# Attention with a fused feed-forward and expert stage: joint transposed tile, paired selector sums, rope sums on another engine

## The chip, the cores and the metric

The kernel runs on one core of a Trainium2 chip. The metric is the device time of one execution in microseconds (us), lower is better. The engines are TensorE (PE in the rows, PEld its weight loads), VectorE (DVE), ScalarE (ACT), GpSimd (POOL) and SyncE (SP, which issues DMAs). Each has its own queue and works through it in order; semaphores hold an instruction until what it needs is there.

## The reference

Three stages follow one another. Only the first is touched; B=4, H=8, S=576, D=64 in fp32:

```
q_rot, k_rot = (rotate(q), rotate(k))           # x1*cos - x2*sin, x1*sin + x2*cos
scores = 1/sqrt(D) * matmul(q_rot, k_rot.T)
scores = scores - max(scores, axis=-1)
attn = exp(scores)
attn = attn / (sum(attn, axis=-1) + 1e-9)
x = matmul(attn, v)                             # 2304 tokens x 512 after the heads are joined
x = moe(x)                                      # RMS norm, silu(x w_gate) * (x w_val), w_out
out = moe2(x)                                   # one of 8 experts per token, relu, gate weight
```

## The kernel before

Attention works on 32 heads `i`, in 16 pairs `p`. A step `g` is one turn of a loop from -25 to 175; a head takes five steps, a pair ten. In each step the list `plan` (L52) is gone through in its order, and each entry (name, offset) calls its method for the head or pair whose time has come: offset -10 means ten steps before the head's first step. So the order of the list is the order of the instructions in every engine's queue within a step, and the offset says in which step. A head's 576 positions are handled as five blocks of rows `j` (four of 128, one of 64).

- `ropeA` multiplies q and k by cosine and sine on GpSimd; `ropeC` (L236) adds the two products, for q on GpSimd, for k on VectorE (`T["rc"]`); `ropeH` (ScalarE, L243) rounds the sum to fp32r, `ropeL` (VectorE, L248) takes the rest, so that both halves together are exact.
- `TQ` (L257) transposes q and k of one head on TensorE, ten transposes into the PSUM tiles `t1` (512 columns each of q and k) and `t2` (64 each). `TE` (L269) copies them to SBUF on ScalarE, k (512 and 64 columns, L274 and L275) and q in turn, and issues the DMAs that make kB and qB.
- `SM` (L286) is one block of scores, row maxima by a reduction on VectorE (L293). `QD` copies the upper half of q by DMA. `MT` (L299) transposes the maxima, ScalarE copies them to `mr`, and a DMA puts them as a row into qB.
- `ST` (L306) is one block of transposed scores, first kA with qA (L317), then kB with qB (L319), the row of maxima being part of qB; ScalarE's exponential (L320) writes it to `E`.
- `AV` (L325) multiplies E with v, `UE` copies the result out. `DN` (L344) sums E over its rows by products with selector matrices: one with `selh` and eight with `sel8`, each in four column tiles of 144 columns. `SQ` does the same for squares. `stat` adds the results, and now and then `wstep` emits small VectorE operations and GpSimd products (L486) that scale what a batch has finished (`ws1` says how many per step). `conv_part` splits weights of the next stage (`cp`).

The score tiles of SM and ST and the tile `t1` come from one PSUM pool, `psA`, with three buffers in rotation; `t2` and MT's tile come from `psC` with one. Before the change AV stands at offset 13 (fourth step of a head), DN at 18, TQ and the two TE in the step at offset -10, ahead of that step's ST.

Of the kernel before, what the change touches and what calls it, by code (L numbers as in the profile page):

```python
# [9 lines left out]
F32 = mybir.dt.float32  # L10
F32R = mybir.dt.float32r
# [6 lines left out]
ALU = mybir.AluOpType  # L18
# [3 lines left out]
B, H, S, D = 4, 8, 576, 64  # L22
NT, DM, DFF = 2304, 512, 1536
P = 128
NPAIR = B * H // 2
NHEAD = B * H
# [5 lines left out]
def fr(ap):  # L32
    return ap.bitcast(F32)
# [16 lines left out]

class Kernel:
    plan = (  # L52
        ("UE1", 20), ("UE0", 15), ("SM", -8), ("AV", 13), ("LV", 1), ("SQ", 23), ("ropeHq", -14), ("TQ", -10),
        ("ropeHk", -13), ("QD", -4), ("TEk", -10), ("ropeLq", -13), ("DN", 18), ("ropeAq", -22), ("ropeAk", -20),
        ("ropeLk", -13), ("LQ", -12), ("MT", -3), ("TEq", -10), ("ropeCk", -15), ("ropeCq", -17), ("ST", 0),
    )


# [207 lines left out]
                nc.tensor.transpose(o, src[:, h * 5 + j].rearrange("p e d -> p (e d)"), self.idr)  # L266
        self.st["t", i] = (t1, t2)

    def TE(self, i, nm):  # L269
        nc, st = self.nc, self.st  # L270
        t1, t2 = st["t", i]
        x = "qk".index(nm)
        dst = self.tp.tile([P, S], F32R, tag=nm + "T", name=nm + "T")
        nc.scalar.copy(dst[:, 0:512], fr(t1[:, x]))  # L274
        nc.scalar.copy(dst[:, 512:576], fr(t2[:, x * 128:x * 128 + 64]))  # L275
        st[nm + "A", i] = dst
        if nm == "q":
            qB = self.tp.tile([P, 640], F32R, tag="qB", name="qB")
            self.dm(qB[0:64, 0:576], dst[64:128])
            st["qB", i] = qB  # L280
        else:
            kB = self.kBt[i % 3]
            self.dm(kB[0:64], dst[0:64])
            st["kB", i] = kB

    def SM(self, i, j):  # L286
        nc = self.nc
# [46 lines left out]
    def UE(self, p, u):  # L334
# [6 lines left out]
            self.st["sq", p] = self.sm.tile([P, S], F32, tag="sq", name="sq")  # L341
        nc.scalar.activation(self.st["sq", p][:, 288 * u:288 * u + 288], av[:, :288], AF.Square)  # L342

    def DN(self, p):  # L344
        nc = self.nc
        b, hp = divmod(p, 4)
        E = self.st["E", p]
        d = self.side(p, 1)
        parts = [(self.selh[:, hp, :], E[:, 0, 4, :])]
        for h in range(2):  # L350
            parts += [(self.sel8[:, 2 * hp + h, :], E[:, h, j, :]) for j in range(4)]
        for x, (w, r) in enumerate(parts):
            for t in range(4):
                nc.tensor.matmul(d[32 * t:32 * t + 32, 0:144], w, r[:, 144 * t:144 * t + 144], start=(x == 0), stop=(x == 8), tile_position=(0, 32 * t))
        self.later.append((b, hp, 0, d))

    def SQ(self, p):
# [141 lines left out]
    def attention(self):  # L499
# [47 lines left out]
        def act(nm, off):  # L547
            if nm in ("UE0", "UE1"):
                ok(self.UE, at(g, off, 10), int(nm[2]))
            elif nm == "ST":  # L550
                ok(self.ST, *divmod(g - off, 5))
            elif nm in ("MT", "TQ", "QD"):
                ok(getattr(self, nm), lagged(nm, off, 5))
            elif nm[:2] == "TE":
                ok(self.TE, lagged("TE", off, 5), nm[2])
            elif nm == "DN":
                ok(self.DN, late(off, self.dnt))
                q = late(off + 1, self.dnt + 1)
                if q >= 0 and q % 4 == 3:
                    wq.append(self.W0(q // 4))  # L560
                if q == 14:
                    wq.append(self.Wa())
            elif nm == "SQ":
                q = late(off, self.sqt)
                ok(self.SQ, q)
                q = late(off + 1, self.sqt)
                if q >= 0 and q % 4 == 3:
                    wq.append(self.W(q // 4))
            elif nm == "SM":
                ok(self.SM, *divmod(g - off, 5))  # L570
            elif nm == "AV":
                if g >= 10 * NPAIR:
                    if g < 10 * NPAIR + 10:
                        self.AV(NPAIR - 1, *divmod(g - 10 * NPAIR, 5))
                elif (g - off) % 5 == 0:
                    p, y = divmod((g - off) // 5, 2)
                    for j in range(5):
                        ok(self.AV, p, y, j)
            elif nm == "LV":
                p = at(g, off, 10)  # L580
                if 0 < p < NPAIR:
                    self.loads(p, "v")
            elif nm == "LQ":
                p = at(g, off, 10)
                if 0 <= p < NPAIR - 2:
                    self.loads(p + 2, "qk")
            elif nm[:4] == "rope":
                ok(getattr(self, nm[:5]), roped(nm, off), nm[5])

# [288 lines left out]
SIZES = (128, 256, 288, 352, 384)  # L878


T = dict(wz=0, pi=8, ck="g", ck8="", c1=0, g0=70, cp=(0, 1, 1, 0, 1, 0, 1, 1, 0, 1), ws1=(0, 1, 2, 2, 1, 0, 1, 1, 2, 1), np=1, w4=3, p0=8, u0=-1, pp=[(1, 1), (1, 3), (2, 1), (2, 3), (3, 1), (3, 3)], w3=4, sqt=12, rc="q", dnt=7, ck2="g", ws=2, ws2=4, u2=1, c2=1, wy=0, yt={0: 1, 2: 1, 3: 2, 4: 1}, yr={0: 2, 2: 2, 3: 1, 4: 1}, bt={1: (0, 1), 2: (2, 2), 3: (3, 3), 5: (4, 5)}, yl={0: 1, 2: 1, 3: 1, 4: 2}, ba={0: (1, 2), 2: (1,), 3: (1,), 4: (1, 3, 5)})


class Ring:
# [752 lines left out]
```

## Time and profile before

| what | us |
|---|---|
| median of 3 runs (1128.01 to 1131.2) | 1130.47 |
| profiled execution | 1130.2 |
| its span, first to last instruction | 1128.4 |
| TensorE busy | 1048.8 (93%) |
| VectorE busy | 655.5 (58%) |
| ScalarE busy | 457.5 (41%) |
| GpSimd busy | 293.2 (26%) |

Attention fills the span from the start to about 350 us, and its last products lie between those of the next stage up to about 377 us. The views are: the page with the busy times; a table of busy time by stretch; the waits, who waited for whom; and the instructions of an engine in order of time. In the order of time a row is: start (us), duration (us), engine, line, operation, output<-input, partitions x elements, count, and in brackets idle time before it and what ended it. A duration runs into that of the next instruction where work is pipelined, so the distance between starts says what an instruction costs its queue.

### The profile page before, as it was taken

How to read it: one execution, taken by the hardware profiler on the slowest of the kernel's cores; microseconds unless marked ns; L12 is line 12 of the kernel's file. 1: busy time of each engine (PE TensorE's matmuls, PEld its weight loads, DVE VectorE, ACT ScalarE, POOL GpSimd, SP SyncE). 2: the span in 40 equal slices, each digit the busy share in tenths (PEclk: the TensorE clock that was granted, in tenths of full speed). 3: DMA queues.
4: the chain of work that ended last, by engine and by line, in shares of the span. 5: the costliest groups of instructions: out<-in, count | busy, mean ns of one | idle time of the engine just before them, and what ended most of it. 6: DMA issues, size and time to landing. Idle time of an engine off the chain costs nothing. (4 is left out here: it accounts for less than half of the span.)

```text
span 1128.4 us, 19271 instructions
## 1 busy us (share of the span) xinstructions
PE 1048.8 (93%) x7174; PEld 891.2 (79%) x7174; DVE 655.5 (58%) x1313; ACT 457.5 (41%) x1023; POOL 293.2 (26%) x357
## 2 busy tenths in 40 slices
PE   3999999999999899999999999999998998899895
PEld 3777777777676689899999999999886887798684
DVE  8554656675642866656565556563457855655653
ACT  2645655655555343322222222222234534434441
POOL 7553356266402401112011011110010132221211
PEclk9999999999998999999999999999999999999998
DMA  4433344335221201111113111100136655655553
GB/s 132 95 86 90 96 119 131 99 106 141 59 74 38 80 16 50 57 47 57 30 62 109 38 48 38 42 25 28 58 125 214 190 188 175 208 185 182 199 189 115
DMA packets 75713, 113.44 MB, mean 101 GB/s; under 512 B 18520, under 2 KB 43376, under 8 KB 75570
## 3 DMA queue, kind: packets, MB, share of 16 engines
q1 hardware_dynamic: 71890, 99.72, 30.1%
q0 software_dynamic: 3680, 11.91, 2.9%
q8 instruction: 78, 1.28, 0.5%
q14 instruction: 65, 0.53, 0.2%
HBM read 85.39 MB, written 12.17 MB: 86 GB/s over the span
## 5 line engine op out<-in xcount | busy, mean ns | idle before, releaser
L760 PE MATMUL gv<-xh,whi 128*128 128x384 f32 x576 | 198.4, 344 | 1.8 <-ACT xh L738 1.4
L760 PE MATMUL gv<-xl,whi 128*128 128x384 f32 x576 | 196.3, 341 | 3.3 <-POOL xl L742 3.1
L760 PE MATMUL gv<-xh,wlo 128*128 128x384 f32 x576 | 196.0, 340 | 0.4 <-POOL wlo L659 0.4
L293 DVE TENSOR_REDUCE m<-s 128x1 fp32r<-128x576 f32 (+1 forms) x160 | 119.9, 752 | 123.8 <-PE s L292 122.6
L320 ACT ACTIVATE E<-sT 128x576 f32<-128x576 f32 (+1 forms) x160 | 104.9, 659 | 137.5 <-PE sT L319 132.0
L659 POOL TENSOR_TENSOR wlo<-cvt,whi 128x256 fp32r<-128x256 f32 x66 | 50.6, 770 | 341.8 <-ACT whi L658 341.8
L770 DVE TENSOR_TENSOR s<-s,gv 128x384 f32<-128x384 f32 x72 | 39.8, 554 | 157.3 <-PE gv L760 150.0
L760 PEld LDWEIGHTS gv<-xh,whi 128*128 128x128 f32 x576 | 109.2, 190 | 8.1 <-issue 3.6
L760 PEld LDWEIGHTS gv<-xl,whi 128*128 128x128 f32 x576 | 109.4, 190 | 5.3 <-POOL xl L742 3.5
L769 ACT ACTIVATE s<-gv 128x384 f32<-128x384 f32 x72 | 34.9, 492 | 192.0 <-PE gv L760 191.9
L760 PEld LDWEIGHTS gv<-xh,wlo 128*128 128x128 f32 x576 | 109.3, 190 | 1.1 <-POOL wlo L659 1.0
L317 PE MATMUL sT<-qT,kT 128*128 128x288 f32 (+1 forms) x320 | 79.9, 332 | 13.0 <-ACT qT L274 13.0
L788 PE MATMUL yps<-whi,hh 128*128 128x512 f32 x216 | 87.3, 404 | 2.9 <-ACT yacc L793 1.4
L331 PE MATMUL av<-E,vraw 128*64 128x288 f32 x640 | 86.5, 414 | 0.8 <-ACT sq L342 0.8
L803 DVE TENSOR_TENSOR yacc<-yacc,yps 128x512 f32<-128x512 f32 x99 | 67.6, 686 | 31.8 <-PE yps L788 30.6
L788 PE MATMUL yps<-wlo,hh 128*128 128x512 f32 x216 | 85.3, 395 | 0.0
L788 PE MATMUL yps<-whi,hl 128*128 128x512 f32 x216 | 85.2, 394 | 0.0
L292 PE MATMUL s<-kT,qT 128*128 128x288 f32 (+1 forms) x320 | 78.2, 330 | 4.9 <-DVE m L293 2.7
L317 PEld LDWEIGHTS sT<-qT,kT 128*128 128x128 f32 (+1 forms) x320 | 47.8, 181 | 30.1 <-ACT qT L274 21.2
L1302 POOL DMA_INDIRECT x<-ysc,ix x27 | 33.0, 1221 | 144.8 <-DVE e L1128 76.7
L319 PE MATMUL sT<-qB,kB 65*128 65x288 f32 (+1 forms) x320 | 69.8, 300 | 0.0
L331 PEld LDWEIGHTS av<-E,vraw 128*64 128x64 f32 x640 | 42.7, 137 | 32.2 <-issue 6.5
(288 smaller groups left out, 1968.6 us busy)
## 6 DMA issues: line engine op xcount, KB each, us to landing
raw<-in_w SPq DMA_DIRECT2D x52, 512.0 KB
stt<-in_w SPq DMA_DIRECT2D x25, 512.0 KB
stt<-in_w_gate SPq DMA_DIRECT2D x24, 256.0 KB
stt<-in_w_val SPq DMA_DIRECT2D x24, 256.0 KB
stt<-in_w_out SPq DMA_DIRECT2D x24, 256.0 KB
kB<-kT SPq DMA_DIRECT2D x32, 144.0 KB
qB<-qT SPq DMA_DIRECT2D x32, 144.0 KB
qT<-qT SPq DMA_DIRECT2D x32, 144.0 KB
```

What stands on the lines that cost most here:

```text
L292: nc.tensor.matmul(s[:n, u, 0:288], qA[:, j * 128:j * 128 + n], kA[:, u * 288:u * 288 + 288], start=True, stop=True)
L293: nc.vector.tensor_reduce(m[:n, j:j + 1], s[:n, :, 0:288], axis=AX.XY, op=ALU.max)
L317: nc.tensor.matmul(s[:n, u, 0:288], kA[:, j * 128:j * 128 + n], qA[:, u * 288:u * 288 + 288], start=True, stop=False)
L319: nc.tensor.matmul(s[:n, u, 0:288], kB[0:65, j * 128:j * 128 + n], qB[0:65, u * 288:u * 288 + 288], start=False, stop=True)
L320: nc.scalar.activation(e.rearrange("p (u c) -> p u c", u=2), s[:n, :, 0:288], AF.Exp, scale=0.125)
L331: self.nc.tensor.matmul(av[64 * h:64 * h + 64, 0:288], V[:, h, j * 64:j * 64 + 64], E[:, h if j < 4 else 0, j, 288 * u:288 * u + 288], sta ...
L659: nc.gpsimd.tensor_tensor(lo, f, fr(hi), op=ALU.subtract)
L760: nc.tensor.matmul(t[:, :CH], w[:, k], r[:, k], start=(n == 0), stop=(n == 11))
L769: nc.scalar.activation(s, ps[0][:, :CH], AF.Silu)
L770: nc.vector.tensor_tensor(s, s, ps[1][:, :CH], op=ALU.mult)
L788: nc.tensor.matmul(ps, l, r[:, 2], start=(n == 0), stop=(n == tot - 1))
L803: nc.vector.tensor_tensor(old[:, t], old[:, t], ps, op=ALU.add)
```

## The change

q and k transposed of a head share one tile `qkT`, and TE makes two copies, of 2 x 512 and of 2 x 64 columns, instead of four. TQ and TE stand at the end of their step, behind ST. `EP` adds E blocks 0 and 1, and 2 and 3, of each head (`es=(0, 1)`; `eg=()` puts both on VectorE), and DN takes the two sums of a head instead of four blocks: five products instead of nine. AV moves from offset 13 to 12 and so ahead of MT and ST of the same step. The rope sum of k goes to GpSimd as that of q does (`rc="qk"`). Offsets and order of the other entries move by a step at most (ropeCk from -15 to -17), and `cp` and `ws1` are dealt out anew: `cp` sums to 6 as before, `ws1` to 13 instead of 11.

```diff
--- before.py
+++ after.py
@@ -50,9 +50,9 @@
 
 class Kernel:
     plan = (
-        ("UE1", 20), ("UE0", 15), ("SM", -8), ("AV", 13), ("LV", 1), ("SQ", 23), ("ropeHq", -14), ("TQ", -10),
-        ("ropeHk", -13), ("QD", -4), ("TEk", -10), ("ropeLq", -13), ("DN", 18), ("ropeAq", -22), ("ropeAk", -20),
-        ("ropeLk", -13), ("LQ", -12), ("MT", -3), ("TEq", -10), ("ropeCk", -15), ("ropeCq", -17), ("ST", 0),
+        ("UE1", 20), ("UE0", 15), ("SM", -8), ("AV", 12), ("SQ", 23), ("ropeCk", -17), ("ropeHk", -14), ("EP0", 10),
+        ("ropeCq", -18), ("QD", -4), ("ropeHq", -14), ("ropeAq", -22), ("EP1", 12), ("ropeLq", -13), ("DN", 18),
+        ("ropeAk", -21), ("ropeLk", -12), ("LQ", -11), ("LV", 1), ("MT", -3), ("ST", 0), ("TQ", -10), ("TE", -10),
     )
 
 
@@ -266,22 +266,17 @@
                 nc.tensor.transpose(o, src[:, h * 5 + j].rearrange("p e d -> p (e d)"), self.idr)
         self.st["t", i] = (t1, t2)
 
-    def TE(self, i, nm):
+    def TE(self, i):
         nc, st = self.nc, self.st
         t1, t2 = st["t", i]
-        x = "qk".index(nm)
-        dst = self.tp.tile([P, S], F32R, tag=nm + "T", name=nm + "T")
-        nc.scalar.copy(dst[:, 0:512], fr(t1[:, x]))
-        nc.scalar.copy(dst[:, 512:576], fr(t2[:, x * 128:x * 128 + 64]))
-        st[nm + "A", i] = dst
-        if nm == "q":
-            qB = self.tp.tile([P, 640], F32R, tag="qB", name="qB")
-            self.dm(qB[0:64, 0:576], dst[64:128])
-            st["qB", i] = qB
-        else:
-            kB = self.kBt[i % 3]
-            self.dm(kB[0:64], dst[0:64])
-            st["kB", i] = kB
+        dst = self.tp.tile([P, 2, S], F32R, tag="qkT", name="qkT")
+        nc.scalar.copy(dst[:, :, 0:512], fr(t1))
+        nc.scalar.copy(dst[:, :, 512:576], fr(t2[:, 0:256]).rearrange("p (x n) -> p x n", x=2)[:, :, 0:64])
+        st["qA", i], st["kA", i] = dst[:, 0], dst[:, 1]
+        kB = st["kB", i] = self.kBt[i % 3]
+        self.dm(kB[0:64], dst[0:64, 1])
+        qB = st["qB", i] = self.tp.tile([P, 640], F32R, tag="qB", name="qB")
+        self.dm(qB[0:64, 0:576], dst[64:128, 0])
 
     def SM(self, i, j):
         nc = self.nc
@@ -341,6 +336,14 @@
             self.st["sq", p] = self.sm.tile([P, S], F32, tag="sq", name="sq")
         nc.scalar.activation(self.st["sq", p][:, 288 * u:288 * u + 288], av[:, :288], AF.Square)
 
+    def EP(self, i, k):
+
+        if k not in T["es"]:
+            return
+        E = self.st["E", i // 2]
+        t = self.st["es", i, k] = self.sm.tile([P, S], F32, tag=f"es{k}", name=f"es{k}", bufs=2)
+        (self.nc.gpsimd if k in T["eg"] else self.nc.vector).tensor_tensor(t, E[:, i % 2, 2 * k, :], E[:, i % 2, 2 * k + 1, :], op=ALU.add)
+
     def DN(self, p):
         nc = self.nc
         b, hp = divmod(p, 4)
@@ -348,10 +351,12 @@
         d = self.side(p, 1)
         parts = [(self.selh[:, hp, :], E[:, 0, 4, :])]
         for h in range(2):
-            parts += [(self.sel8[:, 2 * hp + h, :], E[:, h, j, :]) for j in range(4)]
+            w = self.sel8[:, 2 * hp + h, :]
+            for k in range(2):
+                parts += [(w, self.st.pop(("es", 2 * p + h, k)))] if k in T["es"] else [(w, E[:, h, j, :]) for j in (2 * k, 2 * k + 1)]
         for x, (w, r) in enumerate(parts):
             for t in range(4):
-                nc.tensor.matmul(d[32 * t:32 * t + 32, 0:144], w, r[:, 144 * t:144 * t + 144], start=(x == 0), stop=(x == 8), tile_position=(0, 32 * t))
+                nc.tensor.matmul(d[32 * t:32 * t + 32, 0:144], w, r[:, 144 * t:144 * t + 144], start=(x == 0), stop=(x == len(parts) - 1), tile_position=(0, 32 * t))
         self.later.append((b, hp, 0, d))
 
     def SQ(self, p):
@@ -552,7 +557,7 @@
             elif nm in ("MT", "TQ", "QD"):
                 ok(getattr(self, nm), lagged(nm, off, 5))
             elif nm[:2] == "TE":
-                ok(self.TE, lagged("TE", off, 5), nm[2])
+                ok(self.TE, lagged("TE", off, 5))
             elif nm == "DN":
                 ok(self.DN, late(off, self.dnt))
                 q = late(off + 1, self.dnt + 1)
@@ -584,6 +589,12 @@
                 p = at(g, off, 10)
                 if 0 <= p < NPAIR - 2:
                     self.loads(p + 2, "qk")
+            elif nm[:2] == "EP":
+                q = at(g, off, 5)
+                if q >= NHEAD - 2 or q < 0:
+                    q = g - 10 * NPAIR - 1 + NHEAD - 2
+                    q = q if NHEAD - 2 <= q < NHEAD else -1
+                ok(self.EP, q, int(nm[2]))
             elif nm[:4] == "rope":
                 ok(getattr(self, nm[:5]), roped(nm, off), nm[5])
 
@@ -878,7 +889,7 @@
 SIZES = (128, 256, 288, 352, 384)
 
 
-T = dict(wz=0, pi=8, ck="g", ck8="", c1=0, g0=70, cp=(0, 1, 1, 0, 1, 0, 1, 1, 0, 1), ws1=(0, 1, 2, 2, 1, 0, 1, 1, 2, 1), np=1, w4=3, p0=8, u0=-1, pp=[(1, 1), (1, 3), (2, 1), (2, 3), (3, 1), (3, 3)], w3=4, sqt=12, rc="q", dnt=7, ck2="g", ws=2, ws2=4, u2=1, c2=1, wy=0, yt={0: 1, 2: 1, 3: 2, 4: 1}, yr={0: 2, 2: 2, 3: 1, 4: 1}, bt={1: (0, 1), 2: (2, 2), 3: (3, 3), 5: (4, 5)}, yl={0: 1, 2: 1, 3: 1, 4: 2}, ba={0: (1, 2), 2: (1,), 3: (1,), 4: (1, 3, 5)})
+T = dict(wz=0, pi=8, ck="g", ck8="", c1=0, g0=70, cp=(0, 2, 0, 0, 1, 0, 1, 1, 0, 1, ), ws1=(1, 1, 2, 3, 1, 0, 1, 1, 2, 1, ), np=1, w4=3, p0=8, u0=-1, pp=[(1, 1), (1, 3), (2, 1), (2, 3), (3, 1), (3, 3)], w3=4, sqt=12, rc="qk", es=(0, 1, ), eg=(), dnt=7, ck2="g", ws=2, ws2=4, u2=1, c2=1, wy=0, yt={0: 1, 2: 1, 3: 2, 4: 1}, yr={0: 2, 2: 2, 3: 1, 4: 1}, bt={1: (0, 1), 2: (2, 2), 3: (3, 3), 5: (4, 5)}, yl={0: 1, 2: 1, 3: 1, 4: 2}, ba={0: (1, 2), 2: (1,), 3: (1,), 4: (1, 3, 5)})
 
 
 class Ring:
```

## Rows read from the trace of the kernel before

**Rows 1.** The page: busy time of each engine, share, instructions.

```profile
PE 1048.8 (93%) x7174; PEld 891.2 (79%) x7174; DVE 655.5 (58%) x1313; ACT 457.5 (41%) x1023; POOL 293.2 (26%) x357
```

**Rows 2.** Stretches of one pair: length; PE, PEld, DVE, ACT, POOL; clock; DMA, GB/s.

```profile
83.80:104.60 20.80, 19.72 (x204) 14.90 (x202) 10.10 (x16) 11.64 (x28) 8.95 (x12) 1.00 0.36 87
...
230.20:251.20 21.00, 19.90 (x204) 14.87 (x202) 15.75 (x28) 12.17 (x30) 10.99 (x14) 1.00 0.41 106
...
272.10:293.10 21.00, 19.71 (x204) 14.86 (x202) 11.77 (x17) 12.16 (x30) 18.12 (x25) 1.00 0.28 70
```

**Rows 3.** Waits of TensorE from 62.7 to 314.3 us: total, times, longest.

```profile
PE sT L317 <- ACT qT L274: 11.1, 23, 0.9
PE s L292 <- DVE m L293: 1.8, 8, 0.4
```

**Rows 4.** TensorE in order of time, 200 to 224 us.

```profile
205.07 2.14 PE L354 MATMUL av<-E,sel 128*32 128x144 f32 x64
207.15 0.53 PE L317 MATMUL sT<-qT,kT 128*128 128x288 f32 x2
...
212.48 0.43 PE L292 MATMUL s<-kT,qT 128*128 128x288 f32 x2
212.74 0.22 PE L301 MATMUL t<-idr,m 128*8 128x128 f32 x1
...
213.83 2.65 PE L331 MATMUL av<-E,vraw 128*64 128x288 f32 x20
...
218.69 0.62 PE L266 MATMUL t<-idr,qhl 128*128 128x128 f32 x5
...
219.58 0.50 PE L317 MATMUL sT<-qT,kT 128*128 128x288 f32 x2
...
220.25 0.48 PE L292 MATMUL s<-kT,qT 128*64 128x288 f32 x2
220.94 0.53 PE L317 MATMUL sT<-qT,kT 128*128 128x288 f32 x2 [0.21 <-ACT qT L274]
```

**Rows 5.** VectorE's k sums (ns, min/median/max), the longest, and GpSimd beside it.

```profile
L236 DVE TENSOR_TENSOR A<-A,B x12: 811/815/1380, 73.4 to 303.8; 128x640 f32<-128x640 f32 x12
...
177.43 1.38 DVE L236 TENSOR_TENSOR A<-A,B 128x640 f32<-128x640 f32 x1
...
177.10 2.17 POOL L486 TENSOR_TENSOR x<-x,wb 128x384 f32<-128x384 f32 x2 [3.59 <-DMA wb<-wscr]
```

**Rows 6.** ScalarE in order of time, 200 to 224 us.

```profile
213.22 0.24 ACT L303 CAST mr<-t 8x128 fp32r<-8x128 f32 x1
...
219.70 0.58 ACT L274 CAST kT<-t 128x512 fp32r<-128x512 f32 x1
220.18 0.22 ACT L275 CAST kT<-t 128x64 fp32r<-128x64 f32 x1
...
220.86 0.70 ACT L320 ACTIVATE E<-sT 128x576 f32<-128x576 f32 x1
221.41 0.76 ACT L243 CAST qhl<-A 128x640 fp32r<-128x640 f32 x1
```

**Rows 7.** SP's queue and TensorE in order of time, up to 62 us.

```profile
40.21 0.73 SPq L197 DMA_DIRECT2D qB<-mr  x1
...
43.43 0.50 PE L317 MATMUL sT<-qT,kT 128*128 128x288 f32 x2
```

**Rows 8.** GpSimd's q sum and its reader on ScalarE, 260 to 310 us.

```profile
278.03 1.54 POOL L236 TENSOR_TENSOR A<-A,B 128x640 f32<-128x640 f32 x1
...
284.38 0.73 ACT L243 CAST qhl<-A 128x640 fp32r<-128x640 f32 x1
```

**Rows 9.** TensorE in order of time, up to 62 us.

```profile
26.16 0.85 PE L266 MATMUL t<-idr,qhl 128*128 128x128 f32 x5 [3.23 <-DVE qhl L248]
...
27.80 0.81 PE L317 MATMUL sT<-qT,kT 128*128 128x288 f32 x2
```

**Rows 10.** Busy time and granted clock in one stretch; columns as in rows 2.

```profile
355.00:360.00 5.00, 4.93 (x16) 3.90 (x16) 0.00 (x0) 3.26 (x7) 4.67 (x6) 0.53 0.00 0
```

## The prediction, made before the change was run

> **What bounds the kernel now.** I read the page's busy times first. TensorE is busy for 1048.8 us of 1128.4, 93%, and VectorE for 58% [rows 1]. That is a mean over stages, so the next view is the table by stretch, cut at the start of the transposes of every second head, so that one row is one pair of heads. A quiet pair (83.80 to 104.60) takes 20.80 us: TensorE 19.72, VectorE 10.10, ScalarE 11.64, GpSimd 8.95. The fullest pairs of the other engines are 230.20 to 251.20 (VectorE 15.75 of 21.0) and 272.10 to 293.10 (GpSimd 18.12 of 21.0) [rows 2]. All the change's edits lie in this stage, 16 pairs, and there TensorE is the bound; nobody else comes near except GpSimd in one stretch. The third view says what TensorE's remaining idle time is: in twelve pairs it waits 11.1 us, in 23 places, for the copies of q and k transposed (L274) and 1.8 us, in 8 places, for a maximum (L293) [rows 3]. The fourth, TensorE's order of time, gives prices as distances between starts, because durations overlap [rows 4]. After the attention stage the program is the same in both kernels, and TensorE sets it too; what the stage saves I carry to the end one for one.
>
> **The change part by part.** The sum is made against the profiled execution, 1130.2 us (1.8 over its span of 1128.4), which lies 0.3 under the median, 1130.47.
>
> *Selector products (DN).* Eight products with sel8, each of four tiles side by side, run from 205.07 to 207.15, 2.08 us [rows 4], so 0.26 each. Four of eight go: 1.04 us a pair, on TensorE's own queue with nothing to hide behind. 16 pairs: 16.6 us. In the last pair this lies between products of the next stage, and I count it as well.
>
> *The adds (EP).* 64 adds of 128x576 on VectorE. Not in the trace; the nearest row is the k sum, the same operation on 640 columns: 0.815 us at the median [rows 5], so by columns 0.73 (an estimate). Four a pair are 2.9 us, and the k sum that leaves makes it 2.1 net. 10.10 + 2.1 is 12.2 of about 19 us in a quiet pair, and 15.75 + 2.1 is 17.9 in the fullest [rows 2]. VectorE's queue is in order, so behind each add stands the maximum (L293) that frees a score buffer. The first add of a head stands in the step with the transposes, which give 0.89 us (218.69 to 219.58 [rows 4]) to cover 0.73; the second stands in the step of the AV products, 2.65 us (at 213.83 [rows 4]). DN itself waits for the add of the step before, with AV in between. So I price the adds at 0; without that cover they cost 64 x 0.73 = 47 us.
>
> *Transposes and copies at the end of the step.* Three score buffers rotate, and the transposes take one. Now the second score product behind them (ST of the next step) needs that buffer back; afterwards it is the third (SM of the step after that). In the row: ScalarE is free for the copies at 219.70, the four of them take until the exponential at 220.86, 1.16 us, and ST starts at 220.94, where TensorE was through with SM, which takes 0.26 (212.48 to 212.74), at 220.25 + 0.26 = 220.51 [rows 4, 6]. The stall is 0.43, of which the wait column shows 0.21: it hides about 0.2, so the 23 waits of 11.1 us [rows 3] are about 0.69 each. Afterwards the exponential goes first (0.55, 220.86 to 221.41 [rows 6]). Two copies of 1024 and 128 columns follow; with 0.58 for 512 columns and 0.22 for 64 [rows 6], 0.8 ns a column, the long one is an estimate of 1.0 us, and the buffer is free 0.55 + 1.0 + 0.05 = 1.6 us after ScalarE comes free, where it is 1.2 now. But TensorE reaches the point that needs it later, by one SM (0.26) and one ST (0.67, 219.58 to 220.25): 0.9 us. The merge itself saves ScalarE only 0.1 us, since the small copies ride in the shadow of the large. The stall falls by 0.9 - 0.4 = 0.5 where it is that long: about 0.45 for 28 heads, 12.6 us. From below: nothing, if ScalarE is what sets the pace and the wait just moves one product on. From above: all of it, 24 x 0.69 = 17 us.
>
> *AV before MT.* AV moves one step up, between the third SM and its ST, where TensorE now waits for a maximum: 1.8 us in 8 places [rows 3]; taken as 1.8, between 0 and 1.8. In exchange the row of maxima (MT, its copy mr, its DMA into qB) starts later: from MT to the first ST of that head are 219.58 - 212.74 = 6.84 us now, and without AV (2.65) and the transposes (0.89) 3.3 [rows 4]; the qB product comes 0.3 later, 3.6. The copy ends 0.72 us after MT (213.22 + 0.24 [rows 6]). The DMA's landing has no row; at 40.21 it was issued and at 43.43 + 0.3 the product that needs it ran without a wait [rows 7], so it takes at most 3.5. Chain: at most 4.2 against 3.6, late by 0 to 0.6 in the 16 half pairs that have no DN, 0 to 9 us. I take 0: 2.5 KB inside the chip is nearer to the low end. In SP's queue only the v loads stand newly between kB, qB, QD and this DMA, once a pair.
>
> *Rope sum of k on GpSimd.* 1.54 us a pair there [rows 8], 8.95 to 10.5 of 19 in quiet pairs, and 18.12 to 19.7 in the fullest [rows 2], where the later scaling ops also come closer together. The q sum ends there at 279.57 and its first reader on ScalarE starts at 284.38 [rows 8], 4.8 us of slack against 1.5 for each such pair. 0, and at worst a few us in each of three scaling stretches, 9 in all.
>
> *Start.* TensorE waits 3.23 us before the third head's transposes at 26.16; afterwards the ST that now starts at 27.80 stands ahead of that wait and falls into it; its first half alone lasts 0.81 [rows 9], and with the second I take 1.1 us as saved; the k sum moved to a GpSimd that is full there could eat it, and VectorE free of it could add as much: 0 to 2.2.
>
> **Sum.** 16.6 + 12.6 + 1.8 + 1.1 = 32.1 us. I hold back 2 us for waits that only show when TensorE runs this close: 1130.2 - 32 + 2 = 1100 us.
>
> **A rule against the change.** The row first: the k sum on VectorE has a median of 0.815 us and a maximum of 1.380; that longest one, at 177.43, ran beside a scaling op that GpSimd had begun at 177.10 [rows 5]. So meeting GpSimd costs up to 0.57 us. GpSimd is busy for 8.95 of 20.80 us in a quiet pair [rows 2], so about half of the adds may meet it. The Trainium skill ("SBUF — State Buffer", section "SBUF: two separate sides") says that VectorE instructions with two SBUF inputs and GpSimd instructions lock each other out of a port pair for the whole instruction, which the longest row fits. By that rule the adds and the moved sum make new collisions; the sum above leaves them to VectorE's cover.
>
> **The rivals.** *The copy wait only moves:* ScalarE's order exp, copies, exp sets the pace, and SM inherits the wait. For it: the copies end 0.4 us later than now. Against: TensorE has 0.9 us more until then. Time: 1130.2 - 16.6 - 1.1 = 1112.
>
> *The adds are held up by GpSimd:* each pays the row's 0.57 us; 4 x 0.57 + 17.9 = 20.2 us of VectorE in the three scaling stretches of two pairs, 1 us over TensorE's 19, 6 us together: 1106. In quiet pairs (12.2 + 2.3) it changes nothing. By the rule above it would come out this way.
>
> *GpSimd or the row of maxima comes late:* 9 us of the sum is given back, 1109. Against: the slack of 4.8 us, the small transfer.
>
> *Slower: the adds stand ahead of maxima that TensorE waits for.* Place: VectorE's queue in every step with an add; price 64 x 0.73 = 47 us on TensorE's path, against 32 gained: 1145. It decides once an add holds TensorE up by more than 32 / 64 = 0.5 us. For it: the queue is in order and three buffers are few. Against: the adds have cover of 0.89 and 2.65 us.
>
> *It does not do what it says:* the adds cost what the products save, and the rest hides, 1130.
>
> **How the numbers follow.** Forecast 0.70; wait only moves 0.14; GpSimd lockout 0.05; GpSimd or maxima late 0.05; slower 0.03; nothing 0.03. Range: low, all copy waits gone and the start at its best, 1130.2 - 16.6 - 17 - 1.8 - 2.2 = 1092.6. The clock adds to both sides: in the stretch from 355 to 360 the granted clock was 0.53 [rows 10], right after the stage; whether TensorE's idle time there again lets it fall, and for how long, moves about 3 us. Low 1089. High: only the products gained and 3 us lost, 1112 + 3 = 1115. Inside are the forecast, the moved wait and the two late cases. A measurement of this kernel tells about 0.3%, 3.4 us, from no change: faster 0.94, same 0.03, slower 0.03.
>
> **What would show it.** The pair's stretch falls from 20.8 to about 19.0 us (18.9 quiet); the products with sel8 take 1.04 us; the wait for L274 moves from ST (L317) to SM (L292) and is below 6 us in all; L293's wait does not grow; DN waits for no add; the wait at the third head's transposes shrinks. I am wrong if the pairs stay above 19.7 us, if TensorE waits for maxima or adds by more than 5 us, if the qB products wait for the row of maxima, or if what the pairs save comes back after 340 us.

## The result, and the profile after

| | before | after |
|---|---|---|
| median of the runs side by side, us | 1129.58 (4 runs) | 1114.5 (4 runs, 1110.03 to 1119.26) |
| ratio, 95% interval | | 0.9867 [0.9819, 0.9915] |
| profiled execution, us | 1130.2 | 1116.7 |
| its span, us | 1128.4 | 1115.0 |

Faster by 1.3%, inside the range, but half of what was forecast: the profiled execution is 13.5 us shorter, where 30 were expected. Page of the changed kernel, busy times [rows 1]:

```profile
PE 1037.2 (93%) x6662; PEld 878.8 (79%) x6662; DVE 710.4 (64%) x1362; ACT 459.3 (41%) x959; POOL 331.1 (30%) x372
```

TensorE has 512 instructions less and 11.6 us less to do; VectorE is busy 54.9 us more, GpSimd 37.9 more. The table by stretch of the changed kernel (columns as in rows 2), a quiet pair and the two longest:

```profile
83.86:103.07 19.21, 18.87 (x172) 13.95 (x170) 12.84 (x19) 11.68 (x25) 11.55 (x13) 1.00 0.34 85
...
223.30:246.10 22.80, 19.99 (x172) 15.10 (x171) 20.91 (x30) 12.14 (x25) 15.09 (x16) 0.93 0.37 99
246.10:268.80 22.70, 20.30 (x172) 14.67 (x171) 17.07 (x25) 12.57 (x26) 22.47 (x27) 0.92 0.47 132
```

The quiet pair does what was forecast, nearly: 19.2 us for 20.8. The other two are longer than any pair before was, VectorE is busy for 20.9 of 22.8 us in one of them, and the granted clock is below 1.00, which it is in no stretch of rows 2. Waits of TensorE, 62.7 to 307.9 us (what waited, who released it: total, times, longest) [rows 3]:

```profile
PE sT L312 <- DVE m L288: 5.3, 5, 2.6
...
PE s L287 <- DVE m L288: 1.0, 2, 0.7
PE s L287 <- ACT qkT L273: 0.8, 4, 0.2
```

The 11.1 us for the copies are down to 0.8; the 1.8 for maxima have become 6.3. The longest of these, in the changed kernel's order of time (VectorE, GpSimd and TensorE, 224 to 237 us):

```profile
224.19 1.93 DVE L345 TENSOR_TENSOR es<-E 128x576 f32<-128x576 f32 x1
...
225.46 3.02 POOL L231 TENSOR_TENSOR B<-kraw,cs 128x160 f32<-128x160 f32 x4
...
228.44 3.75 POOL L236 TENSOR_TENSOR A<-A,B 128x640 f32<-128x640 f32 x2
...
229.35 1.45 DVE L345 TENSOR_TENSOR es<-E 128x576 f32<-128x576 f32 x1
...
230.72 1.63 DVE L462 TENSOR_TENSOR y<-y,ms 128x144 f32<-128x144 f32 x1
...
232.62 0.75 DVE L288 TENSOR_REDUCE m<-s 128x1 fp32r<-128x576 f32 x1
...
233.42 0.48 PE L312 MATMUL sT<-qkT 128*64 128x288 f32 x2 [2.57 <-DVE m L288]
...
235.80 0.83 PE L266 MATMUL t<-idr,khl 128*128 128x128 f32 x5
236.44 0.70 PE L287 MATMUL s<-qkT 128*64 128x288 f32 x2
```

GpSimd works without a gap until 232.19. Beside it an add takes 1.93 and 1.45 us, and one multiplication of 144 columns 1.63, ending 0.16 us after GpSimd does. The maximum behind them starts at 232.62, TensorE waits 2.57 us for it, and after that its clock falls: the five transposes of k, 0.43 from start to start in a quiet pair (84.24 to 84.67), take 0.64 (235.80 to 236.44). The changed kernel's adds and maxima from 62 to 308 us (ns, min/median/max) say which instructions suffer:

```profile
L345 DVE TENSOR_TENSOR es<-E x48: 736/800/1927, 62.9 to 301.1; 128x576 f32<-128x576 f32 x48
...
L288 DVE TENSOR_REDUCE m<-s x121: 683/757/759, 62.2 to 307.5; 128x1 fp32r<-128x576 f32 x97, 64x1 fp32r<-64x576 f32 x24
```

The adds read and write SBUF alone; the maxima read PSUM, and not one of 121 is stretched.

### The profile page after: what moved, and what is told of

It is laid out like the page before. It is cut to its first block, busy times and chain, and to the rows that moved or that the text cites. A ratio compares the mean times of both kernels' runs of the same rounds, so it can differ in the third digit from the quotient of the medians.

```text
span 1115.0 us, 18245 instructions
## 1 busy us (share of the span) xinstructions
PE 1037.2 (93%) x6662; PEld 878.8 (79%) x6662; DVE 710.4 (64%) x1362; ACT 459.3 (41%) x959; POOL 331.1 (30%) x372
## 5 line engine op out<-in xcount | busy, mean ns | idle before, releaser
L312 PE MATMUL sT<-qkT 128*128 128x288 f32 (+1 forms) x320 | 80.6, 334 | 10.2 <-DVE m L288 6.1
L287 PE MATMUL s<-qkT 128*128 128x288 f32 (+1 forms) x320 | 79.6, 335 | 6.6 <-ACT qkT L273 2.7
L1313 POOL DMA_INDIRECT x<-ysc,ix x27 | 30.3, 1121 | 143.1 <-DVE e L1139 76.7
L1432 POOL DMA_INDIRECT out<-cvt,ix x20 | 25.3, 1265 | 156.1 <-DVE cvt L1430 120.2
```

Source lines behind the costliest of these rows:

```text
L287: nc.tensor.matmul(s[:n, u, 0:288], qA[:, j * 128:j * 128 + n], kA[:, u * 288:u * 288 + 288], start=True, stop=True)
L312: nc.tensor.matmul(s[:n, u, 0:288], kA[:, j * 128:j * 128 + n], qA[:, u * 288:u * 288 + 288], start=True, stop=False)
```

## The experiments

The following table is worked out from the starts of the transposes of every second head, as the stretches of rows 2 are (us): the quiet pair is the one from about 84; pairs 2 and 3 lie between about 42 and 84; pair 6 begins near 122; pairs 10 to 12 are those from 202 to 269 in the changed kernel; then the start of the last pair, and the time before it in which the granted clock stood at its lower level, 1.2 GHz. Pairs are counted from 0. Each row is one execution, and executions of one kernel lie up to 12 us apart (e10), so that small differences may be chance. The runs e3 and e7 show how much: up to 124 us they have the changed kernel's instructions, and pairs 2 and 3 took 39.9 and 40.8 us in them, 41.7 in the changed kernel.

| kernel | quiet | 2 and 3 | 6 | 10 to 12 | last pair | lower clock |
|---|---|---|---|---|---|---|
| before | 20.8 | 41.3 | 20.9 | 63.1 | 314.3 | 0 |
| after | 19.2 | 41.7 | 21.1 | 66.7 | 307.9 | 17.1 |
| e1 | 20.2 | 39.9 | 21.0 | 64.4 | 316.6 | 10.2 |
| e2 | 19.6 | 40.0 | 21.2 | 64.6 | 306.9 | 6.8 |
| e3 | 19.2 | 39.9 | 21.8 | 67.1 | 308.9 | 13.7 |
| e4 | 19.2 | 41.5 | 21.5 | 65.7 | 306.9 | 17.1 |
| e5 | 19.2 | 43.1 | 23.8 | 59.6 | 306.2 | 10.2 |
| e6 | 20.3 | 42.7 | 20.6 | 64.1 | 313.6 | 10.2 |
| e7 | 19.2 | 40.8 | 21.6 | 67.6 | 309.1 | 20.5 |
| e8 | 19.2 | 43.6 | 23.7 | 59.8 | 306.9 | 10.2 |
| e9 | 19.2 | 37.9 | 21.2 | 62.5 | 297.0 | 3.4 |
| e10 | 19.2 | 38.3 | 22.0 | 62.5 | 313.3 | 17.1 |
| e11 | 19.2 | 38.6 | 21.7 | 62.6 | 313.2 | 17.1 |
| e12 | 19.4 | 40.2 | 20.5 | 59.7 | 304.8 | 17.1 |

Letters of theories belong to the expectation they stand in. The first four runs ask which part of the change lengthens the busy pairs.

**e1, no adds.** Nine products again, all else as changed.

```diff
-es=(0, 1, )
+es=()
```

> The changed kernel without its adds: nine selector products again, all else as changed. The changed kernel took 1114.5 us; its quiet pairs of heads take 19.2 us (20.8 before), but the pairs from 202 to 268 us take 21.2, 22.8 and 22.7 (21.2, 21.0, 20.9 before). Theory A (VectorE is too full in the scaling stretches and at the start, and the adds fill it): quiet pairs 20.2 to 20.3, and the three pairs fall to 20.5 to 21.0 in spite of 1.0 us more of products; TensorE's waits for maxima (L288), 5.3 us and 1.0 us now, fall below 2; time 1113 to 1119, about the changed kernel's. Rival B (the moved k sum or the denser scaling makes those waits, not the adds): the three pairs stay at 22 or more and the time rises by the 16 us of the products, to 1128 to 1133.

Measured: 1122.08 us, ratio to before 0.9935 [0.9908, 0.9961]. So adds and products are worth 7.7 us together by the ratios, give or take 6, not 16.6. In quiet pairs they are worth all of it (20.2 to 19.2). Pairs 10 to 12 together are 2.3 us shorter without the adds, though they have 3 us more of products, so the adds are a part of the cause; but one of these pairs still takes 22.5, so they are not all of it, and neither forecast came out. One pair, of 26.2 us, shows the rest at its plainest. (This execution took 1128.1 us, 6 more than the median of the run, so the pair is an example and not the rule.) Run without adds, order of time, 163 to 175 us:

```profile
163.90 4.63 POOL L491 TENSOR_TENSOR x<-x,wb 128x384 f32<-128x384 f32 x6
...
166.71 6.88 DVE L676 TENSOR_SCALAR ct<-ct 128x256 f32<-128x256 f32 x1 [1.20 <-ACT ct L694]
168.46 1.57 POOL L224 TENSOR_TENSOR A<-qraw,cs 128x640 f32<-128x640 f32 x1
...
169.97 1.97 POOL L231 TENSOR_TENSOR B<-qraw,cs 128x160 f32<-128x160 f32 x4
171.88 1.56 POOL L491 TENSOR_TENSOR x<-x,wb 128x384 f32<-128x384 f32 x2
173.51 1.41 DVE L288 TENSOR_REDUCE m<-s 128x1 fp32r<-128x576 f32 x2
...
174.31 0.85 PE L312 MATMUL sT<-qkT 128*128 128x288 f32 x2 [4.08 <-DVE m L288]
```

A conversion that takes 0.29 us alone takes 6.88: it ends at 173.59, just behind GpSimd's unbroken row of 13 instructions (173.44). The maximum behind it frees a score buffer, TensorE waits 4.08 us, and the lower clock follows. From here on theory G: VectorE's SBUF-only instructions are held up by GpSimd, in a queue in which the maxima stand behind them.

**e2, k sum on VectorE.**

```diff
-rc="qk"
+rc="q"
```

> The changed kernel with the rope sum of k back on VectorE. Theory A (VectorE's fill): 0.73 us more a pair on VectorE, the pairs from 202 to 268 us no shorter than 21.2, 22.8 and 22.7, time 1114 to 1120. Rival B (the k sum on GpSimd keeps GpSimd busy beside VectorE's two-input operations and stretches them): those pairs fall to 20.5 or less, the half-clock stretch that begins at 40.9 us goes, the subtractions at the start (1.4 to 1.8 us each now) fall to about 0.8, time 1103 to 1109.

Measured: 1116.51, 0.9862 [0.9825, 0.9899], the same as the changed kernel. It gains 2.1 in pairs 10 to 12 (64.6) and loses 0.4 in each quiet pair; its 40.0 in pairs 2 and 3 is what e3 and e7 take there with the k sum on GpSimd, so no gain at the start is shown. Neither forecast came out: the three pairs take 21.2 to 21.8. The moved sum costs nothing in all, as I priced it, but only as a balance.

**e3, the old spread.**

```diff
-ws1=(1, 1, 2, 3, 1, 0, 1, 1, 2, 1, )
+ws1=(0, 1, 2, 2, 1, 0, 1, 1, 2, 1, )
```

> The changed kernel with the scaling operations spread as before (11 instead of 13 in ten steps). Theory A: the same work on VectorE over a little more time; the pairs from 202 to 268 us lose less than 1 us each, time 1111 to 1116. Rival S (the denser spread makes the waits): those pairs fall to 20.0 to 20.5, time 1105 to 1109.

Measured: 1118.93, 0.9883 [0.9844, 0.9922]. Pairs 10 to 12 stay at 67.1: the denser spread is not the cause.

**e4, narrow scaling products.**

```diff
-                    (nc.gpsimd if T["np"] else V).tensor_tensor(x, x, w[:, hp, q0:q1], op=ALU.mult)
+                    x = x[:, 0:8]
+                    (nc.gpsimd if T["np"] else V).tensor_tensor(x, x, w[:, hp, q0:q0 + 8], op=ALU.mult)
```

> The changed kernel with GpSimd's scaling products cut to 8 columns each, so that most of x stays unscaled: the experts' share of tokens changes, and only the attention stage's rows are to be read, not the time. Theory A1 (VectorE operations are stretched by GpSimd's scaling products beside them): adds in the stretch from 223 to 268 us fall from up to 1.9 us to 0.75 to 1.1, the 128x144 operations from up to 1.6 to 0.3, and the pairs there from 22.8 and 22.7 to 19.5 to 20.5. Theory A2 (VectorE's own number of operations is what fills it): the adds stay as they are or the pairs stay above 21.5.

One execution, to be read up to 310 us, since most of x stays unscaled: the last of pairs 10 to 12 fell from 22.7 to 20.9, as A1 said; the one before took 23.6 (22.8 in the changed kernel), with a wait of 2.53 for a maximum. There it is the rope work that meets VectorE, not the scaling.

**e5, early conversions.**

```diff
-g0=70, cp=(0, 2, 0, 0, 1, 0, 1, 1, 0, 1, )
+g0=30, cp=(0, 0, 0, 0, 2, 1, 2, 1, 0, 0, )
-            if 20 <= g < 24:
-                self.att_const2(g - 20)
+            if 24 <= g < 28:
+                self.att_const2(g - 24)
```

> The weight conversions (L676 to L682, steps 1, 4, 6, 7, 9 from g = 70 on) start at g = 30 and stand in steps 4 to 7 only, where GpSimd has no rope work; the constants of L180 move from g = 20..23 to 24..27. Theory G (VectorE instructions that touch only SBUF are stretched while GpSimd works, the maxima behind them in the queue come late, and the clock halves): the stretch from 202.1 to 268.8 us, 66.7 us in the changed kernel, falls to about 62, with no half clock in it; the second pair (62.7 to 83.8, 21.1) loses 1.5 us; the pairs from 84 to 145 stay within 0.5 us; in all about 1109. Theory S (GpSimd's own work in that stretch, 15.1 and 22.5 us of a pair, is what comes late): the stretch stays above 65.5 us, and the time is 1114 or more.

Measured: 1116.16, 0.9872 [0.9847, 0.9897]. Pairs 10 to 12 fell by 7.1 us, more than G asked, with GpSimd's rope and scaling work unchanged: S falls. (The later weight loads left this stretch too, so G is not alone in this gain; e9 parts them.) But the time is the same, for the loss moved. In pair 6 (23.8) the conversions now meet the reciprocal square root, and pairs 2 and 3 grew by 1.4. Run with early conversions, SP's queue and TensorE, 53 to 63 us:

```profile
53.22 0.59 SPq L197 DMA_DIRECT2D qB<-qkT  x1
53.87 2.05 SPq L645 DMA_DIRECT2D stt<-in_w_gate  x2
...
55.97 0.98 SPq L645 DMA_DIRECT2D stt<-in_w_val  x2
57.47 0.50 SPq L197 DMA_DIRECT2D qkT<-qkT  x1
...
62.62 0.58 PE L312 MATMUL sT<-qkT 128*128 128x288 f32 x2 [2.57 <-DMA qkT<-qkT]
```

The first four weight loads (256 KB each) are issued ahead of the copy of q's upper half (QD), and TensorE waits 2.57 us for that copy. That is a second cause, theory L. The changed kernel has such a wait at 142.71 (1.25 us), with the same loads issued from 134.90 to 137.06 and QD at 137.16; the trace puts it down to VectorE's L456, which happened to end last, but e9 names QD's copy at the same place. The clock falls behind it there as well (143.2). The kernel before issues the same loads ahead of QD too (137.73 to 139.88, QD at 139.99) and waits for nothing there, because the product that needs the copy comes 7.2 us after QD's issue (147.21). In the changed order, with ST ahead of the transposes and fewer selector products, TensorE is there after 4.3 us (141.46). So the wait is the change's own doing.

**e6, the adds alone.** The kernel before, with the adds and the five products of the change and nothing else of it.

```diff
-("SQ", 23), ("ropeHq", -14),
+("SQ", 23), ("EP0", 10), ("ropeHq", -14),
-("QD", -4), ("TEk", -10),
+("QD", -4), ("EP1", 12), ("TEk", -10),
```

> The kernel before, with the adds (EP0 at 10, EP1 at 12) and the five products in place of nine as its only change. By the prediction's term for the products: 16.6 us faster than before. Theory G: the quiet pairs fall from 20.8 to 19.8 us, but the pairs in which GpSimd runs scaling operations keep their 21 us or grow, so that half of the 16.6 us is left: 7 to 9 us faster than before, as the difference between the changed kernel and the one without adds says (7.6). Theory B (the copies' stall hides the products): the quiet pairs stay above 20.3 us.

Measured: 1129.16, 0.9996 [0.9977, 1.0015]: nothing. Quiet pairs fall by 0.5 only (G had 1.0), and the busy ones take that back. By its number, above 20.3, theory B came out, but not by its mechanism: the waits for copies are 2.4 us in three quiet pairs, 2.7 in the kernel before. Waits of TensorE in this run, three quiet pairs (84.4 to 145.6):

```profile
PE sT L317 <- ACT qT L274: 2.4, 6, 0.6
PE s L292 <- DVE m L293: 1.3, 3, 0.5
```

In the half pair without DN an add beside GpSimd's multiplications took 2.11 us (85.32), the maximum behind it started at 87.35, and TensorE waited 0.44 for it (88.15): once a pair. In the changed kernel the add that is held in a quiet pair (1.09 us at 87.31) lies beside the AV products (86.53 to 89.11), and nothing waits behind it. So the 0.98 us a pair is there only together with the rest of the change; the parts do not add up.

**e7, scaling on VectorE.**

```diff
-np=1
+np=0
```

> The changed kernel with the scaling products of L491 on VectorE instead of GpSimd (np = 0): 24.5 us of GpSimd's work go, some 9 us of VectorE's (by columns, from the k sum's 0.815 us for 640) are added. Theory G (meeting GpSimd is the cost, not VectorE's sum): the stretch from 202.1 to 268.8 us falls by 2 us or more, most in its last pair (22.7), though VectorE has more to do. Theory A (VectorE's sum of work, 20.9 of 22.8 us in the fullest pair, is the bound): the stretch grows by 2 us or more.

Measured: 1116.69, 0.9879 [0.9856, 0.9902]. Pairs 10 to 12 grew by 1.0, between the two forecasts, so the run doesn't decide. The last of them fell from 22.7 to 22.1 though VectorE had more to do; the one before rose from 22.8 to 24.3, with 10.2 us at the lower clock instead of 3.4.

**e8, early conversions, and the k sum of p = 1 to 3 on VectorE.** e5's edit, and in `ropeC`:

```diff
-        (self.nc.gpsimd if p and nm in T["rc"] else
+        (self.nc.gpsimd if p > (3 if nm == "k" else 0) and nm in T["rc"] else
```

> As the run with early conversions, and the k sum of the first three pairs back on VectorE. Theory G: the first two pairs come out as with the k sum on VectorE throughout (15.7 and 19.2 us, no half clock at 41), quiet pairs stay at 19.2, and the time is 2 to 3 us under the run with early conversions alone, about 1106. Rival (the two gains don't add up, since the time lost at the start is covered later): the same as that run, within 1 us.

Measured: 1116.83, 0.9885 [0.9857, 0.9912]; pair 2 takes 22.5 (19.2 was expected) with the same loads in the way. The rival was right: the gains don't add up.

**e9, GpSimd nearly idle.** e4's edit, and from the second pair on the sine products and the rope sums cover 8 columns:

```diff
+                if p:
+                    e.tensor_tensor(o[:, h, 0, y, 0:8], r[:, h, 0, 1 - y, 0:8], s5[:, 0, y, 0:8], op=ALU.mult)
...
+            self.nc.gpsimd.tensor_tensor(A[:, x, 0:8], A[:, x, 0:8], Bt[:, x, 0:8], op=ALU.add)
```

> The changed kernel with GpSimd's sine products, rope sums and scaling products cut to 8 columns from the second pair on (so q and k lack most of their sine part, the scaling is left out, the output is another and tokens are routed otherwise: only the attention stage up to 310 us can be read). VectorE, TensorE and ScalarE have the same work as in the changed kernel. Theory G (VectorE is held up by GpSimd's trains): the pairs that take 21.1 to 22.8 us in the changed kernel come out at 19.2 to 19.8, no half clock between 80 and 290 us, the last pair starts near 296 in place of 307.9, and VectorE's adds have no instance over 0.8 us away from the two multiplications that are left. Theory A (VectorE's sum of work as it is without GpSimd): these pairs stay above 20.5 us.

One execution. The last pair starts at 297.0, 10.9 us earlier, with VectorE's work the same: 0.9 of it by the start of pair 1 (25.0 for 25.9), 5.6 in the next three pairs, 4.4 after them. (Between 1 and 2 of the 5.6 may be chance: e3 and e7, with the changed kernel's instructions, take 2.1 and 1.2 us less than it for these pairs.) Its adds from 62 to 297 us:

```profile
L351 DVE TENSOR_TENSOR es<-E x47: 739/748/2052, 62.9 to 290.3; 128x576 f32<-128x576 f32 x47
```

The median is the undisturbed 0.75 now. Less work on GpSimd also makes its own results ready earlier, but that can hardly be the gain behind the start of pair 1: in the changed kernel's profile no wait of TensorE, VectorE or ScalarE between 25 and 345 us is ended by GpSimd. Theory G holds for the total, not for every pair: three pairs stay above 21 us, and the clock is low once, where none was expected. One (pair 6) has the wait for QD behind the weight loads, 1.39 us at 136.29. In the next, from 195.44, the multiplications left to GpSimd meet the reciprocal square root (order of time, both engines and TensorE):

```profile
213.57 1.55 POOL L224 TENSOR_TENSOR A<-qraw,cs 128x640 f32<-128x640 f32 x1
...
213.73 1.55 DVE L460 TENSOR_TENSOR y<-y 128x144 f32<-128x144 f32 x1
...
216.01 0.53 PE L318 MATMUL sT<-qkT 128*128 128x288 f32 x2 [1.16 <-DVE m L294]
```

L460 takes 0.31 alone. The third, from 236.4, has a wait of 0.92 us at 246.59 for the row of maxima, whose DMA stands behind a weight load (243.72), and the lower clock from 247.5 on. So of the three, two are SP's queue and one is what is left of GpSimd's work.

**e10 and e11, into GpSimd's gaps.** The constants move to g = 23 to 26 besides; e11 also has the k sum of p = 1 and 2 on VectorE.

```diff
-g0=70, cp=(0, 2, 0, 0, 1, 0, 1, 1, 0, 1, )
+g0=60, cp=(0, 0, 0, 2, 2, 2, 2, 2, 0, 0, )
-ws1=(1, 1, 2, 3, 1, 0, 1, 1, 2, 1, )
+ws1=(0, 0, 0, 1, 3, 3, 3, 3, 0, 0, )
```

> The changed kernel with VectorE's other work put where GpSimd has none: conversions from g = 60 on, two pieces in each of the steps 3 to 7; the constants of L180 at g = 23 to 26; the steps of the reciprocal square root and the scaling in steps 3 to 7 only. Theory G: the stretch from 202 to 269 us falls from 66.7 to about 60 as with the early conversions, the pair that begins near 122 us, which grew to 23.8 there because conversions met the reciprocal square root, stays below 20.5; time about 1106, 10 us under the changed kernel. Rival (each such move only shifts the meeting to another pair, as the early conversions did): within 3 us of the changed kernel.

> As the run before it, and the k sum of the second and third pair on VectorE. Theory G: the first two pairs at 15.7 and 19.2 us without a half clock at 41 us, 1 to 2 us less than that run. Rival: no difference.

Measured: 1125.19, 0.9948 [0.9926, 0.997], and 1125.82, 0.9948 [0.992, 0.9975]: 10 us worse than the changed kernel, and e11 no better. Run e10, two pairs and the one behind them:

```profile
186.40:211.60 25.20, 19.58 (x172) 14.40 (x171) 22.07 (x27) 13.28 (x29) 24.11 (x28) 0.96 0.42 106
211.60:235.70 24.10, 22.31 (x174) 16.27 (x173) 17.64 (x28) 11.77 (x25) 15.21 (x17) 0.83 0.32 82
235.70:254.90 19.20, 18.88 (x172) 14.00 (x171) 14.23 (x24) 11.69 (x25) 10.77 (x12) 1.00 0.40 93
```

The scaling came later and met the conversions in one pair: GpSimd was busy for 24.1 of 25.2 us there, so it had no gap left. Where neither stands, pairs take 19.2. And TensorE waited 3.23 us for QD behind the weight loads at 121.11. A gap found in one schedule isn't there once the work has moved.

**e12, loads apart.** The weight loads one by one, behind the row of maxima; no conversions where the reciprocal square root stands:

```diff
-            if g == T["g0"] - 15:
-                self.conv_loads()
-            if T["g0"] <= g < 10 * NPAIR and self.cj[0] < 6:
+            if g in (12, 17, 22, 27):
+                self.conv_load(self.cl)
+                self.cl += 1
+            if T["g0"] <= g < 10 * NPAIR and g // 10 != 5 and self.cj[0] < 6:
```

with `g0=30, cp=(0, 0, 0, 0, 2, 2, 2, 2, 0, 0)` and the constants at g = 23 to 26.

> The changed kernel with its first four weight loads (L645, issued together between a head's qB copy and its QD copy on SP's queue) issued one by one at g = 12, 17, 22 and 27, behind the row of maxima; conversions from g = 30, two pieces in each of the steps 4 to 7, none in g = 50 to 59, where the reciprocal square root stands; the constants of L180 at g = 23 to 26. Theory L (the four loads hold up QD's copy of q: 2.6 us at 65 us in the run with early conversions, 3.2 us at 121 us in the run with the work in the gaps, and the 1.25 us at 142.7 in the changed kernel, each followed by half clock): the pair before 63 us, 21.7 with early conversions, comes out below 20, no wait for that copy is above 0.5 us, no half clock before 80 us. With theory G the pair from about 122 us, 23.8 there, comes out at 21 or less and the stretch of three pairs from 202 on stays near 59.5. Time about 1108, 7 to 9 us under the changed kernel. Rival (the meetings move again): within 3 us of the changed kernel.

Measured: 1112.7, 0.9829 [0.9801, 0.9856]. Among the waits from 26 to 305 us none for QD is left, so L's mechanism holds, and pair 6 and pairs 10 to 12 came out as G said. But the pair before 63 us took 20.5, where L had below 20, with the lower clock from 40.8 on after waits of 0.80 and 0.46, just as in the changed kernel; e3 and e7 take 18.7 there with the changed kernel's instructions, so this pair says nothing on L's price. By the ratios this is 4 us under the changed kernel, but the intervals overlap: no proven gain over it, where 7 to 9 us were expected. The meeting is now between 101 and 166 us; run e12, order of time:

```profile
114.53 1.59 POOL L224 TENSOR_TENSOR A<-qraw,cs 128x640 f32<-128x640 f32 x1
114.75 1.65 DVE L680 SCALAR_TENSOR_TENSOR ct<-stt,ct 128x256 int32<-128x256 int32 x1
...
119.31 1.73 POOL L224 TENSOR_TENSOR A<-kraw,cs 128x640 f32<-128x640 f32 x1
...
120.22 1.50 DVE L248 TENSOR_TENSOR khl<-A,khl 128x640 fp32r<-128x640 f32 x1
...
122.44 0.64 PE L312 MATMUL sT<-qkT 128*128 128x288 f32 x2 [1.07 <-DVE m L288]
```

## Why the prediction was half right

**What held.** TensorE was the bound of the quiet pairs, and the products were worth what [rows 4] said. The changed kernel's quiet pair:

```profile
84.24 0.59 PE L266 MATMUL t<-idr,khl 128*128 128x128 f32 x5
84.67 0.43 PE L287 MATMUL s<-qkT 128*64 128x288 f32 x2
85.14 0.53 PE L312 MATMUL sT<-qkT 128*128 128x288 f32 x2
85.50 0.42 PE L314 MATMUL sT<-qB,kB 65*128 65x288 f32 x2
86.04 0.56 PE L287 MATMUL s<-qkT 128*128 128x288 f32 x2
...
99.42 1.16 PE L359 MATMUL av<-es,sel 128*32 128x144 f32 x32
100.52 0.53 PE L312 MATMUL sT<-qkT 128*128 128x288 f32 x2
```

The four products with sel8 take 1.10 us (99.42 to 100.52), 0.98 less than in [rows 4]; 1.04 was the term. The wait for the copies moved to SM and is 0.8 us in all, as the list said; DN waits for no add; the wait of 3.23 at the third head [rows 9] is gone, though the stage comes only 0.2 us earlier there, not 1.1, since the ST in front of it waits 1.33 for QD (24.32).

**Copies: the term was twice too large.** In the same half pair of the kernel before, the stall behind the transposes was 0.71 us (from 85.31 + 0.26 to 86.28):

```profile
85.31 0.43 PE L292 MATMUL s<-kT,qT 128*64 128x288 f32 x2
86.28 0.54 PE L317 MATMUL sT<-qT,kT 128*128 128x288 f32 x2 [0.54 <-ACT qT L274]
```

The changed kernel, ScalarE:

```profile
84.42 0.66 ACT L315 ACTIVATE E<-sT 128x576 f32<-128x576 f32 x1
```

Here ScalarE is free at 84.42 and the buffer 1.6 us later, at 86.04, exactly as worked out. But TensorE comes at 85.50 + 0.26 = 85.76 and waits 0.28, and it has already lost 0.20 ahead of ST (0.47 from 84.67 to 85.14, where 0.27 is the work), which now waits for the exponential in front of the copies, the one that I moved there and charged to nobody. So 0.48 of the 0.71 stayed, 0.23 was saved, where I had 0.45. SM directly before SQ or DN, as it stands now, takes 0.36 between starts (89.77 to 90.13), 0.1 more than elsewhere (91.16 to 91.42). With AV's move all of it is 0.6 a pair in e1 (20.8 to 20.2), where I had 1.03. Over 14 pairs, 2.07 - 1.56 = 0.5 each, 7 us of the miss.

**The busy pairs: the step that failed.** The step is "So I price the adds at 0", with 17.9 us of VectorE in the fullest pair of about 19: it summed durations from quiet rows. In the busy pairs of the changed kernel TensorE waits for the maxima instead, 6.3 us in all with a single wait of 2.57. The prediction had the row against it, the k sum of 1.38 us beside GpSimd [rows 5], and the rival built on it. The mechanism of that rival was right and its size was wrong, in three ways. It charged the adds only, but any VectorE instruction that touches SBUF alone can pay, and VectorE's 25 to 32 instructions in such a pair hold many. It charged 0.57 each, but one was held for 1.2 (adds of 1.93 us), 1.3 (L462) and, in e1, 6.6. And it charged VectorE's sum, where the price is paid in the queue: a maximum that stands behind one such instruction is late at once, long before VectorE is full. To this comes the clock, which I had only for 3 us at the end of the stage [rows 10]: 17.1 us at the lower level. There work takes 0.64 for 0.43, so about a third of it is lost, 5.7 us (an estimate from these two rows).

**SP's queue: seen, and priced at 0.** I named the v loads that stand newly ahead of the row of maxima, and gave its lateness 0.05. The weight loads, which come by in the same queue, I did not count, nor that ST, moved ahead of the transposes, would want QD's copy sooner. The changed kernel, SP's queue, ScalarE and TensorE, 251 to 257 us:

```profile
251.91 0.25 ACT L298 CAST mr<-t 8x128 fp32r<-8x128 f32 x1 [2.06 <-issue]
...
252.84 1.14 SPq L192 DMA_DIRECT2D vraw<-in_v  x2
...
254.08 0.53 SPq L645 DMA_DIRECT2D stt<-in_w_val  x1
...
254.71 0.77 SPq L197 DMA_DIRECT2D qB<-mr  x1
...
256.93 0.50 PE L314 MATMUL sT<-qB,kB 65*128 65x288 f32 x2 [1.46 <-issue]
```

The row is copied by 252.16, but its DMA is issued 2.55 us later, behind v and a weight load, and the qB product waits 1.46 us; at 259.3 the clock is low. It happens once, in the longest pair but one; pair 6, 1.8 us over the quiet pairs, has the wait for QD in the same queue. The sign "if the qB products wait for the row of maxima" stood in my list.

**The sum.** By the start of the last pair I had 14 x 2.07 + 1.1 = 30.1 us, and 6.4 came. 7 of the 23.7 missing is the size of the copies' term and of AV's move. Of the other 16.6, e9 gives 10.9 back by taking GpSimd's work away alone. Its two pairs with SP's queue (21.2 and 21.5) lie 4.3 over the quiet 19.2. The last 1.4 is within what I can't part: the meetings that e9 leaves, and differences between executions, which are as large. After the last pair's start the span gained 7.0 us where I had 2.1, which brings the total back: 3.1 of it is the stretch of AV behind the last score product, of which 1.0 is that pair's shorter sums; in the rest the kernel before had the clock at 0.53 [rows 10] and the changed kernel has not. That the median then lies inside the range, 0.5 us under its upper end, is luck: that end was worked out for a copy wait that only moves, while the busy pairs took most of what is missing, and the profiled execution lies above it.

**The rule.** The Trainium skill ("SBUF — State Buffer", section "SBUF: two separate sides") says that a VectorE instruction with two SBUF inputs, or in a two-port mode, and a GpSimd instruction shut each other out for a whole instruction. By e1's row and e9 that side of it agrees, and it should have had the larger chance; whether e1's conversion, with one input, ran in such a mode no trace shows. The measured hold is longer than one instruction, though: 6.88 us, across eight GpSimd instructions or more, none of which took 1.6.

**The slower rival.** "The adds stand ahead of maxima that TensorE waits for" was given 0.03, since the adds had cover. In the old order (e6) one add of the four of a pair does hold TensorE up, by 0.44 us: 0.11 an add, far from the 0.5 an add at which that rival decided. Alone the adds so cost about what the products save, and the time is that of the last rival, 1130. The change escapes that by what else it moves.

## What to carry to other kernels

Before putting work on VectorE beside a busy GpSimd, list VectorE's instructions that touch only SBUF, with their longest and not their median durations, and look at what stands behind each in the queue: a maximum that frees a buffer pays for the whole hold. A quiet stretch prices a change only for quiet stretches; each of the others needs its own row. And try parts together as well as alone: here, by the ratios, the adds alone gave nothing, all else alone 7 us, both together 15.

## What the runs showed of the hardware

- A VectorE TENSOR_SCALAR of 128x256 in SBUF, 0.29 us alone, took 6.88 us beside an unbroken row of GpSimd instructions and ended 0.15 us after it (e1). In the changed kernel all 121 maxima that read PSUM stayed within 0.76 us.
- Waits of TensorE as short as 1.2 us (142.71, changed kernel), and of 0.80 and 0.46 close together (39.49 and 40.98, e12), were followed by the lower clock; in e1 a wait of 4.08 by 6.8 us of it. But waits of 0.96 and 0.47 at the same place in e7 (39.39 and 40.85) were not, nor one of 1.15 in the changed kernel (222.69).
- Behind four loads of 256 KB in SP's queue, QD's copy could be used 5.15 us after its issue began (57.47 to 62.62, e5).
